# A spectral transformer block of eight batches: the second batch's attention begins beside the first batch's spectral part

## The chip, the cores and the metric

The kernel runs on one core of a Trainium2 chip. The metric is the device time of one execution in microseconds; of the kernel before the median of three runs is given. The engines are TensorE (PE, with its weight loads as PEld), VectorE (DVE), ScalarE (ACT), GpSimd (POOL) and SyncE (SP), whose queue issues the transfers. Each works off its own queue in order.

## The reference

```python
def _attn_ref(q, k, v, g_q, g_k):          # 8 batches, 12 heads, 448 positions, 64 per head
    q_n, k_n = rmsnorm(q, g_q), rmsnorm(k, g_k)
    scores = q_n @ k_n.transpose(0, 1, 3, 2) / sqrt(64)
    attn = exp(scores - max); attn = attn / (sum + 1e-9)
    return attn @ v

def _moe_ref(x, w_ch1, w_ch2):             # x: the heads side by side, 8 x 448 x 768
    mixed = real(fft(fft(x, axis=1), axis=2))
    u = x + mixed
    un = (u - mean(u)) / sqrt(var(u) + 1e-6)
    return u + relu(un @ w_ch1) @ w_ch2    # 768 x 3072 and 3072 x 768; both arrive as 64-bit floats
```

## The kernel before

A batch goes through four parts. **Attention** takes the heads in six pairs: normalise q and k (`norm_pair`), transpose them (`transpose_pair`, products `qk`), then four rows of scores of 112 positions each (`softmax_pair`: products `S`, minimum `mn`, exponential into `P`, sum, scaling), then transposes of `P` (`pt`, copied to SBUF as `T`) and products with the values (`av`) into `xT` (`value_pair`). **Spectral**: `fold` adds and subtracts halves and thirds of `xT` on VectorE (`eo`, `sd`, `tot`), `spectral` does the two transforms as products with the tables `D1` (products `y`, split into `Y`) and `D2` (products `ab`), adds transposes of `xT` (`x`) into `u` and normalises to `un`. **Input**: `ffn_input` transposes `un` into `unT`. **Feed-forward**: 24 `up` steps (products `h`, 18 each) and 36 `down` steps (products `o`, 12 each), 864 products a batch, in the order up 0, then six times four ups and six downs.

Most operands are split into a high and a low part, `A.copy` for the high and a subtraction for the low, so that three fast products stand for one exact one. In the first six pairs (batch 0) attention runs in plain 32-bit instead, without that split (`PLAIN_PAIRS`); the copies `T` of `pt` alternate there between VectorE and ScalarE.

The weights arrive in 64 bits. `convert` turns a tile into two 32-bit parts: a load into a raw slot (tile `dblw...`, slots `X`), two ScalarE steps (L653 into `magw...`, slot `M`; L654), three VectorE steps (L655, L659, L663), GpSimd's addition (L667), ScalarE's copy into the high part (L668), GpSimd's subtraction into the low part (L669). `Stream.converted` does a tile in two halves; there are two `M` slots of a whole tile each and four raw slots of half a tile. 60 tiles (24 for `up`, of 768 columns; 36 for `down`, of 512) are converted once and kept in DRAM: 14 during the first batch's attention and spectral part (`convert_some`, names with an `e`), the rest when `W1.load` or `W2.load` comes to them in the first feed-forward. Each stream has three buffers.

The program first issues all of batch 0's attention and spectral part. Then, for each batch, `merge` walks the feed-forward and, beside it, attention and spectral part of the next batch (`aux`): each `yield` carries a cost in ns, and the side advances until its costs reach a ratio of the main's. A scheduler with a time model of its own then moves instructions within each queue. `order` binds an instruction behind another: `pace` keeps the feed-forward's products in order, and `follow` puts batch 1's score products behind the last feed-forward product issued before them.

PSUM has eight banks: two for `ffn`, two for `S`, two for `PT`, one each for `av` and `q`; in batch 0 `y` uses `S` and `PT`, and `ab` uses `S`.

## Time and profile before

| | |
|---|---|
| median of 3 runs | 2242.81 us (2241.82 to 2243.02) |
| profiled execution, its own time | 2246.45 us |
| its span | 2244.7 us |
| TensorE busy | 2107.8 us (94%) |
| VectorE busy | 1630.5 us (73%) |
| ScalarE busy | 1074.2 us (48%) |
| GpSimd busy | 576.2 us (26%) |
| mean granted TensorE clock | 0.96 |

The profile is of one execution. Busy shares are means over parts with different limits: up to 197 us there is no feed-forward, from 197 to 546 us there is the first one with the conversion of the weights, and from there on seven feed-forwards with kept weights. A number after an instruction is its source line; operations called through a recording helper all have line 111 there, so they are told apart by the names of their tiles.

### The profile page before, as it was taken

The numbers are of one execution on the slowest core, as the hardware profiler recorded it, in microseconds if no ns is written. First come the engines' busy times: TensorE is split into PE (matmuls) and PEld (weight loads), VectorE is DVE, ScalarE is ACT, GpSimd is POOL, SyncE is SP. The second block draws the span as 40 slices with busy tenths as digits, with TensorE's granted clock in tenths as the row PEclk, the third lists the DMA queues.
The fourth block names the chain that finished last, engine by engine and source line by source line (L and its number), as shares of the span: only waits on it lengthen the run. The fifth ranks groups of instructions, "written<-read, shape, count | busy, mean of one in ns | idle before, by whom it ended". The sixth has DMA issues, their size and how long they took to land.

```text
span 2244.7 us, 32045 instructions
## 1 busy us (share of the span) xinstructions
PE 2107.8 (94%) x11164; PEld 1854.6 (83%) x11164; DVE 1630.5 (73%) x3281; ACT 1074.2 (48%) x2452; POOL 576.2 (26%) x442
## 2 busy tenths in 40 slices
PE   6887987769999999999999999999999999998997
PEld 3346866668999999999999999999999999998996
DVE  6896999888888577866788587867787588752122
ACT  5766776656554255524554355524554355421100
POOL 5883666854122021211121021101221022000000
PEclk7987988889999999999999999999999999999998
DMA  4556565557655575557655675558556674549664
GB/s 127 174 158 234 174 200 190 200 193 261 201 177 177 185 230 166 179 174 224 189 173 180 200 216 164 177 175 240 179 163 183 206 213 157 177 145 263 211 209 136
DMA packets 299188, 425.38 MB, mean 190 GB/s; under 512 B 187489, under 2 KB 225362, under 8 KB 299026
## 3 DMA queue, kind: packets, MB, share of 16 engines
q1 hardware_dynamic: 299026, 423.32, 61.0%
q8 instruction: 89, 1.46, 0.3%
q14 instruction: 73, 0.60, 0.1%
HBM read 363.47 MB, written 65.27 MB: 191 GB/s over the span
## 4 chain that ended last, share of the span: by engine, by line
PE 79%; DVE 9%; DMA 3%; ACT 2%; issue 2%; POOL 2%; SPq 0%; DVEq 0%; POOLq 0%; ACTq 0%
PE h L853 29%; PE o L874 28%; PE S L350 6%; PE av L439 4%; PE pt L427 4%; PE qk L313 1%; DMA w<-w 1%; PE y L530 1%; DVE mn L111 1%; DVE magw L663 1%; DMA dblw<-w 1%; PE oT L819 1%; DVE T L111 1%; DVE magw L655 1%; PE un L765 1%
## 5 line engine op out<-in xcount | busy, mean ns | idle before, releaser
L874 PE MATMUL o<-hs,w 128*128 128x448 f32 x3456 | 801.7, 374 | 24.5 <-DVE magw L655 6.8
L853 PE MATMUL h<-unT,w 128*128 128x448 f32 x3456 | 782.7, 371 | 6.0 <-POOL w L669 5.4
L874 PEld LDWEIGHTS o<-hs,w 128*128 128x128 f32 x3456 | 646.1, 191 | 84.0 <-ACT w L668 10.2
L853 PEld LDWEIGHTS h<-unT,w 128*128 128x128 f32 x3456 | 639.8, 189 | 59.7 <-POOL w L669 6.1
L111 ACT ACTIVATE P<-S,mn 112x448 f32<-112x448 f32 x384 | 243.1, 634 | 214.4 <-DVE mn L111 200.8
L111 POOL TENSOR_TENSOR qkn<-raw 112x1024 f32<-112x1024 f32 x47 | 89.8, 1912 | 731.1 <-PE qk L313 558.4
L111 DVE TENSOR_REDUCE mn<-S 112x1 f32<-112x448 f32 x384 | 233.3, 617 | 49.4 <-PE S L350 46.3
L111 ACT ACTIVATE hs<-h 128x448 fp32r<-128x448 f32 x192 | 104.4, 544 | 291.3 <-PE h L853 290.4
L111 DVE TENSOR_TENSOR acc<-o,acc 128x448 f32<-128x448 f32 x240 | 148.9, 621 | 109.5 <-PE o L874 107.8
L111 DVE SCALAR_TENSOR_TENSOR hs<-h,hs 128x448 fp32r<-128x448 f32 x192 | 119.3, 622 | 128.7 <-ACT hs L111 126.8
L439 PE MATMUL av<-T,vhl 128*128 128x448 f32 x504 | 179.9, 391 | 21.1 <-DVE T L111 11.6
L111 ACT CAST T<-pt 128x448 fp32r<-128x448 f32 x252 | 132.9, 533 | 135.3 <-PE pt L427 133.2
L111 POOL TENSOR_TENSOR ss<-ss,nhalf 112x16 f32<-112x16 f32 x48 | 150.0, 3125 | 112.9 <-DVE ss L111 109.6
L111 DVE TENSOR_TENSOR T<-pt,T 128x448 fp32r<-128x448 f32 x252 | 154.7, 617 | 27.8 <-ACT T L111 26.4
L111 DVE TENSOR_SCALAR P<-P,sm 112x448 f32<-112x448 f32 x336 | 158.0, 504 | 4.4
L427 PE MATMUL pt<-ident,P 112*128 112x112 f32 x1008 | 146.8, 262 | 1.5 <-DVE acc L111 1.5
L111 POOL TENSOR_TENSOR rstd<-st,nhalf 112x1 f32<-112x1 f32 (+2 forms) x32 | 18.5, 577 | 489.3 <-DVE st L111 489.3
L427 PEld LDWEIGHTS pt<-ident,P 112*128 112x128 f32 x1008 | 122.9, 143 | 23.0 <-DVE acc L111 2.1
L350 PE MATMUL S<-KD,QT 128*112 128x448 f32 x352 | 137.8, 393 | 2.0 <-ACT KD L111 1.6
L350 PE MATMUL S<-KL,QT 128*112 128x448 f32 x352 | 131.5, 376 | 2.6 <-DVE KL L111 2.5
L439 PEld LDWEIGHTS av<-T,vhl 128*128 128x128 f32 x504 | 95.7, 192 | 32.8 <-DVE T L111 14.9
L667 POOL TENSOR_TENSOR magw<-magw,dblw 128x256 uint32<-128x256 uint32 (+1 forms) x92 | 87.2, 956 | 73.6 <-DVE magw L663 50.4
(121 smaller groups left out, 2689.2 us busy)
## 6 DMA issues: line engine op xcount, KB each, us to landing
w<-w SPq DMA_DIRECT2D x288, 512.0 KB, 4.1
w<-w SPq DMA_DIRECT2D x192, 768.0 KB, 4.4
dblw<-w SPq DMA_DIRECT2D x60, 256.0 KB, 2.9
dblw<-w SPq DMA_DIRECT2D x32, 384.0 KB, 3.9
raw<-q SPq DMA_DIRECT2D x96, 112.0 KB, 4.3
raw<-k SPq DMA_DIRECT2D x96, 112.0 KB, 3.9
v<-v SPq DMA_DIRECT2D x96, 96.0 KB, 3.5
u_dram<-u SPq DMA_DIRECT2D x24, 336.0 KB, 3.5
```

The costliest lines, as they stand in the source:

```text
L111: ins = emit(*args, **kwargs)
L313: nc.tensor.transpose(pt[:, c * C : (c + 1) * C], qk[:, i, c].rearrange("t h d -> t (h d)"), ident[:C, :C],)
L350: ins = nc.tensor.matmul(s_, QT[:, h, cs], K[:, h], start=step == 0, stop=step == 1)
L427: nc.tensor.transpose(pt[:, c * C : (c + 1) * C], Pc[c][:, 512 * h + j * 128 : 512 * h + (j + 1) * 128], ident[:C, :C],)
L439: nc.tensor.matmul(av[:, :S], lv, T[:, i], start=(j == 0 and i == 0), stop=False)
L530: nc.tensor.matmul(o, src[:, par, t0 : t0 + n], D1[:, ri, par, cols], start=i != 1, stop=i != 0,)
L655: behind(nc.vector.tensor_scalar(out=value, in0=value, scalar1=MIN_HIGH, scalar2=MAX_HIGH, op0=ALU.max, op1=ALU.min,))
L663: behind(nc.vector.scalar_tensor_tensor(out=bits, in0=high, scalar=0xC0000000, in1=bits, op0=ALU.bitwise_and, op1=ALU.bitwise_or,))
L667: behind(nc.gpsimd.tensor_tensor(out=bits, in0=bits, in1=low, op=ALU.add))
L765: nc.tensor.transpose(pt[:, OFFS[i] : OFFS[i] + LENS[i]], uns[i][:, p * 128 : (p + 1) * 128], ident[: LENS[i], : LENS[i]],)
L853: pace(nc.tensor.matmul(o, w[:, a, c], unT[c][:, z], start=n == 0, stop=n == 17))
L874: pace(nc.tensor.matmul(o, w[:, a, f], hs[4 * g + f][:, z], start=n == 0, stop=n == 11))
```

## The change

Five things are edited. (1) The side work of batch 1 starts early: while batch 0 is in its spectral part, each of its steps is followed by two steps of batch 1, up to 14 (`AHEAD`). These 14 steps hold the four rows of scores of batch 1's first pair, and the transposes of q of its second. (2) `follow` now applies to all of batch 1's side products but the transposes of attention, and two `yield`s of 7000 and 1500 ns are added in its spectral part. (3) The transform's tables are loaded at step 40 of batch 0 instead of after its first step, the second one in two transfers; the gains' loads are issued in front of the first pair's. (4) In the plain pairs all copies `T` go to ScalarE. (5) A weight tile is converted whole: raw slots are twice as wide and two instead of four. `KL` and `D2` share one tile, and `xT` is allocated later.

```diff
+DFT_STEP = 40
+AHEAD = 14
...
-    def follow(ins):
-        order(
-            ins, paced[-1], mybir.DependencyClass.NoSync, mybir.DependencyReason.DATA
-        )
+    def follow(b, ins):
+        if b == 1 and paced:
+            order(
+                ins, paced[-1], mybir.DependencyClass.NoSync,
+                mybir.DependencyReason.DATA,
+            )
...
-    SLOTS = {"P": 8, "PT": 6, "X": 4, "M": 2, "unT": 6, "h": 6}
+    SLOTS = {"P": 8, "PT": 6, "M": 2, "unT": 6, "h": 6}
+    def wide(name, dtype=F32):
+        return sb.tile([128, 1800], dtype, tag="X", name=name, bufs=2)
...
         st = slot("PT", "d2s")[:N1, : 4 * N1].rearrange("s (n t) -> s n t", n=4)
-        nc.sync.dma_start(st, d2.rearrange("s (n t) -> s n t", n=4))
+        for r in rows_of(N1):
+            nc.sync.dma_start(st[r], d2[r].rearrange("s (n t) -> s n t", n=4))
...
-                    if (h * 3 + j) % 2 == 0:
-                        V.tensor_copy(T, pt[:, :S])
-                    else:
-                        A.copy(T, pt[:, :S])
+                    A.copy(T, pt[:, :S])
...
+                if b == 1:
+                    yield 400
                 for i in range(2):
-                    nc.tensor.matmul(
+                    follow(b, nc.tensor.matmul(
                         av[:, :S], lv, T[:, i], start=(j == 0 and i == 0), stop=False
-                    )
-                yield 800
+                    ))
+                yield 400 if b == 1 else 800
...
         a_, b_, c_ = EO
+        if b == 1:
+            yield 7000
...
             yield 980
+            if b == 1:
+                yield 1500
             for mirror in range(2):
...
-        raw = slot("X", f"dbl{name}", U32)[:, : c * f].rearrange(
+        raw = wide(f"dbl{name}", U32)[:, : c * f].rearrange(
...
-            for c in (slice(0, self.n // 2), slice(self.n // 2, self.n)):
-                convert(
-                    src[:, c], bits[:, c], [hl[:, k, c] for k in range(2)],
-                    f"{self.tag}{name}_{c.start}",
-                )
+            convert(src, bits, [hl[:, k] for k in range(2)], f"{self.tag}{name}")
...
+    load_gains()
     load_pair(0, 0)
-    load_gains()
     warm()
-    side = aux(0)
-    next(side)
-    load_dft()
-    for _ in side:
-        convert_some(CONVERT_EARLY)
+    second = aux(1)
+    ahead = iter(range(AHEAD if nb > 1 else 0))
+    for n, _ in enumerate(aux(0)):
+        if n == DFT_STEP:
+            load_dft()
+        if mixing:
+            for _ in range(2):
+                if next(ahead, None) is not None:
+                    next(second)
+        if n:
+            convert_some(CONVERT_EARLY)
...
-            aux(b + 1) if b + 1 < nb else iter(()),
+            second if b == 0 else aux(b + 1) if b + 1 < nb else iter(()),
```

`mixing` gets an entry when `aux` of a batch passes from attention to the spectral part. The products `y`, `x` and `ab` are wrapped in `follow` like `av`.

How the built queues move, at three places. The head of VectorE's queue; `0_0` is batch 0, pair 0. Before:

```order
L111 TENSOR_REDUCE ss0_0_139<-qkn0_0_137 112x16
L111 TENSOR_TENSOR raw0_0_110<-raw0_0_110,gneg_75 112x512
L111 TENSOR_SCALAR ss0_0_139<-ss0_0_139 112x16
L111 TENSOR_TENSOR D2_78<-d2s_159,D2_78 113x4x113
L111 TENSOR_TENSOR qkn0_0_137<-raw0_0_110,ss0_0_139 112x2x4x64 x2
L111 TENSOR_TENSOR QT0_0_163<-qk0_0_0_165,QT0_0_163 64x448 x2
```

and in the changed kernel:

```order
L113 TENSOR_REDUCE ss0_0_137<-qkn0_0_135 112x16
L113 TENSOR_TENSOR raw0_0_112<-raw0_0_112,gneg_75 112x512
L113 TENSOR_SCALAR ss0_0_137<-ss0_0_137 112x16
L113 TENSOR_TENSOR qkn0_0_135<-raw0_0_112,ss0_0_137 112x2x4x64 x2
L113 TENSOR_TENSOR QT0_0_156<-qk0_0_0_158,QT0_0_156 64x448 x2
```

The subtraction that makes the low part of `D2` no longer stands between the mean squares `ss` and the scaling `qkn`.

ScalarE's queue where the first batch's `Y` are copied (first two digits of `Y`: batch, real or imaginary; of `P`, `mn`, `S`: batch, pair, row). Before:

```order
L668 CAST w1e5_1379<-magw1e5_1380 128x384 x2
L668 CAST w1e6_1468<-magw1e6_1469 128x384 x2
L111 CAST Y0_0_0_1498<-y0_0_0_1491 113x390
L654 ACTIVATE dblw2_6_0_2185<-dblw2_6_0_2185 128x256
L111 CAST Y0_0_1_1508<-y0_0_1_1501 112x390
L654 ACTIVATE dblw2_6_2_2195<-dblw2_6_2_2195 128x256
L111 CAST Y0_1_0_1518<-y0_1_0_1511 113x390
L111 CAST Y0_1_1_1528<-y0_1_1_1521 112x390
L111 COPY bs0_0_1539<-ab0_0_1_1535 113x390
```

and in the changed kernel:

```order
L694 CAST w1e5_1269<-magw1e5_1270 128x768
L113 ACTIVATE P1_0_0_1371,sm1_0_0_1373<-S1_0_0_0_1374,mn1_0_0_1372 112x448
L113 CAST Y0_0_0_1368<-y0_0_0_1361 113x390
L113 CAST Y0_0_1_1395<-y0_0_1_1388 112x390
L694 CAST w1e6_1348<-magw1e6_1349 128x768
L113 ACTIVATE P1_0_0_1371,sm1_0_0_1373<-S1_0_0_1_1375,mn1_0_0_1372 112x448
L113 ACTIVATE P1_0_1_1398,sm1_0_1_1400<-S1_0_1_0_1401,mn1_0_1_1399 112x448
L680 ACTIVATE dblw2_6_2107<-dblw2_6_2107 128x512
L113 ACTIVATE P1_0_0_1371<-P1_0_0_1371,sm1_0_0_1373 112x448
L113 ACTIVATE P1_0_1_1398,sm1_0_1_1400<-S1_0_1_1_1402,mn1_0_1_1399 112x448
L113 CAST Y0_1_0_1422<-y0_1_0_1415 113x390
L113 CAST Y0_1_1_1432<-y0_1_1_1425 112x390
```

Exponentials and scalings of batch 1's first rows stand among the `Y` casts, and the step on the raw tile `dblw2_6` has moved from behind the first cast to behind the second.

VectorE's queue around one weight tile of the first feed-forward, `w1_10`. Before:

```order
L111 RECIPROCAL sm1_2_0_2317<-sm1_2_0_2317 112x2
L655 TENSOR_SCALAR magw1_10_2503<-magw1_10_2503 128x384 x2
L111 TENSOR_SCALAR P1_2_0_2315<-P1_2_0_2315,sm1_2_0_2317 112x448
L659 TENSOR_SCALAR magw1_10_2503<-magw1_10_2503 128x384 x2
L111 TENSOR_TENSOR xT1_1752<-av1_0_1_2114,xT1_1752 64x448
L663 SCALAR_TENSOR_TENSOR magw1_10_2503<-dblw1_10_0_2504,magw1_10_2503 128x384
L111 TENSOR_TENSOR R1_1_2382<-rem1_1_2377,R1_1_2382 64x448
L663 SCALAR_TENSOR_TENSOR magw1_10_2503<-dblw1_10_3_2514,magw1_10_2503 128x384
L111 TENSOR_TENSOR T1_1_0_0_2393<-pt1_1_0_0_2388,T1_1_0_0_2393 128x448
```

and in the changed kernel:

```order
L113 TENSOR_TENSOR T1_1_1_0_2379<-pt1_1_1_0_2374,T1_1_1_0_2379 128x448
L681 TENSOR_SCALAR magw1_10_2405<-magw1_10_2405 128x768
L685 TENSOR_SCALAR magw1_10_2405<-magw1_10_2405 128x768
L113 TENSOR_SCALAR sm1_2_3_2307<-sm1_2_3_2307 112x2
L689 SCALAR_TENSOR_TENSOR magw1_10_2405<-dblw1_10_2406,magw1_10_2405 128x768
L113 RECIPROCAL sm1_2_3_2307<-sm1_2_3_2307 112x2
```

Six instructions with three others among them have become three with one.

## Rows read from the trace of the kernel before

**Rows 1.** Stretches: us, busy us of each engine (instructions), PEclk, DMA share, GB/s.

```profile
20.00:154.00 134.00, 114.38 (x416) 49.69 (x416) 121.60 (x254) 106.09 (x264) 103.95 (x76) 0.84 0.53 158
154.00:197.00 43.00, 22.61 (x101) 19.22 (x102) 31.20 (x62) 16.86 (x36) 24.32 (x20) 0.58 0.56 183
197.00:237.00 40.00, 40.00 (x214) 36.25 (x214) 28.34 (x60) 30.33 (x71) 14.90 (x13) 0.98 0.66 215
237.00:500.00 263.00, 200.29 (x946) 171.54 (x945) 241.76 (x468) 177.50 (x423) 180.30 (x167) 0.86 0.59 192
500.00:546.00 46.00, 42.24 (x228) 37.18 (x227) 39.67 (x96) 30.35 (x76) 25.04 (x34) 1.00 0.80 283
546.00:795.00 249.00, 249.00 (x1392) 227.98 (x1391) 188.48 (x382) 116.74 (x263) 39.14 (x22) 1.00 0.62 189
```

The engines stand in the order PE, PEld, DVE, ACT, POOL.

**Rows 2.** Timeline, 5 to 21 us: start, us, engine, line, operation [idle before, releaser].

```profile
5.84 0.39 SPq L191 DMA_DIRECT2D d2s<-d  x1
...
10.82 2.93 POOL L111 TENSOR_TENSOR ss<-ss,nhalf 112x16 f32<-112x16 f32 x1 [8.72 <-DVE ss L111]
18.63 0.57 ACT L111 CAST D<-d2s 113x452 fp32r<-113x452 f32 x1 [16.61 <-DMA d2s<-d]
...
19.78 1.29 DVE L111 TENSOR_TENSOR qkn<-raw,ss 112x512 f32<-112x512 f32 x2
```

**Rows 3.** Groups, 20 to 154 us: count, busy us, mean ns of one, idle before.

```profile
L111 ACT ACTIVATE P<-S,mn 112x448 f32<-112x448 f32 x48 | 30.2, 631 | 10.4 <-DVE mn L111 10.3
L111 DVE TENSOR_REDUCE mn<-S 112x1 f32<-112x448 f32 x48 | 28.5, 614 | 1.5 <-PE S L347 1.4
...
L111 DVE COPY T<-pt 128x448 f32<-128x448 f32 x18 | 11.1, 616 | 6.2 <-PE pt L396 6.2
...
L111 ACT COPY T<-pt 128x448 f32<-128x448 f32 x18 | 9.5, 527 | 1.4 <-PE pt L396 1.3
```

**Rows 4.** Timeline of VectorE, 369 to 397 us: single instructions and pairs.

```profile
370.04 0.49 DVE L659 TENSOR_SCALAR magw<-magw 128x256 uint32<-128x256 uint32 x2
...
390.31 0.35 DVE L655 TENSOR_SCALAR magw<-magw 128x384 f32<-128x384 f32 x1
...
396.18 0.61 DVE L655 TENSOR_SCALAR magw<-magw 128x384 f32<-128x384 f32 x2
```

**Rows 5.** Timeline of ScalarE in the spectral part of batch 0.

```profile
173.62 0.43 ACT L654 ACTIVATE dblw<-dblw 128x256 uint32<-128x256 uint32 x1 [2.81 <-DMA dblw<-w]
...
174.91 0.85 ACT L111 CAST Y<-y 113x390 fp32r<-113x390 f32 x2
```

**Rows 6.** From the chain of waits: one run of feed-forward products.

```profile
542.98 2.45 PE o L874 x12
```

**Rows 7.** Groups, 237 to 500 us: GpSimd's addition and ScalarE's step on the raw tile.

```profile
L667 POOL TENSOR_TENSOR magw<-magw,dblw 128x256 uint32<-128x256 uint32 x42 | 37.5, 902 | 28.5 <-DVE magw L663 19.1 <-DMA raw<-k 4.4 <-DVE sm L111 2.6
...
L667 POOL TENSOR_TENSOR magw<-magw,dblw 128x384 uint32<-128x384 uint32 x32 | 36.1, 1133 | 31.1 <-DVE magw L663 25.6 <-ACT w L668 2.3 <-ACT dblw L654 1.5
...
L654 ACT ACTIVATE dblw<-dblw 128x256 uint32<-128x256 uint32 x41 | 17.8, 437 | 14.0 <-DMA dblw<-w 12.3 <-DVE qkn L111 0.9 <-DVE eo L111 0.6
```

**Rows 8.** Timelines of ScalarE and GpSimd: tile w1_10 from first to last, and a wait.

```profile
259.46 0.98 ACT L653 ACTIVATE magw<-dblw 128x384 f32<-128x384 f32 x2
...
270.12 2.10 POOL L669 TENSOR_TENSOR w<-magw,w 128x384 fp32r<-128x384 f32 x2
...
489.12 0.44 ACT L653 ACTIVATE magw<-dblw 128x256 f32<-128x256 f32 x1 [1.23 <-POOL w L669]
```

**Rows 9.** The page's transfers: count, KB each, median us to landing.

```profile
dblw<-w SPq DMA_DIRECT2D x60, 256.0 KB, 2.9
dblw<-w SPq DMA_DIRECT2D x32, 384.0 KB, 3.9
```

**Rows 10.** Waits of TensorE, 237 to 500 us: total, times, longest.

```profile
PE y L530 <- DVE eo L111: 14.7, 1, 14.7
```

More of the change, by code (lines that the diff above doesn't have):

```diff
@@ L165, in rows_of @@
         return [slice(a, z) for a, z in ((0, n - n % 16), (n - n % 16, n)) if a < z]
-    KL = cpool.tile([128, 2, S], F32R, name="KL")
+    rounded = cpool.tile([128, 2 * S + 8 * N1], F32R, name="rounded")
+    KL = rounded[:, : 2 * S].rearrange("r (h t) -> r h t", h=2)
     G.memset(KL.bitcast(F32), 0.0)
@@ L199, in spectral_block @@
     X_BANKS = (("either", "either"), ("either", "either"))
-    FOLD_SLOTS = (("unT", "unT"), ("PT", "P"), ("M", "X"))
+    FOLD_SLOTS = (("unT", "unT"), ("PT", "P"), ("M", None))
     loaded = {}
@@ L352, in softmax_pair @@
                     )
-                    if b == 1 and step == 0 and paced:
-                        follow(ins)
+                    if step == 0:
+                        follow(b, ins)
             for h, s_ in enumerate(banks):
@@ L448, in value_pair, with attention @@
         A.copy(xT[:, p, S : S + 1], xT[:, p, 0:1])
-    def attention(b, xT, EO):
+    xTs = {}
+    def attention(b, EO):
         yield from transpose_pair(b, 0)
@@ L468, in attention @@
             if p > 3 and b != 1:
-                fold(b, p - 4, xT, EO)
+                fold(b, p - 4, xTs[b], EO)
                 yield 0
-            values = value_pair(b, p, Pc, xT)
+            if p == 0:
+                xTs[b] = sb.tile([128, NR, S + 2], F32, tag="xT", name=f"xT{b}", bufs=1)
+            values = value_pair(b, p, Pc, xTs[b])
             for x in ahead:
@@ L475, in attention @@
         for p in range(0 if b == 1 else 2, 3):
-            fold(b, p, xT, EO)
+            fold(b, p, xTs[b], EO)
             yield 0
     rstds = {}
+    halves = {}
     def fold(b, p, xT, EO):
@@ L487, in fold @@
         once = slot(short, f"sd{b}_{p}").rearrange("r (i e t) -> r i e t", i=2, e=2)
-        eo = slot(kept, f"eo{b}_{p}").rearrange("r (i t) -> r i t", i=2)
+        if kept is not None:
+            eo = slot(kept, f"eo{b}_{p}")
+        else:
+            if p % 2 == 0:
+                halves[b] = wide(f"eo{b}_{p}")
+            eo = halves[b][:, p % 2 * 900 : p % 2 * 900 + 900]
+        eo = eo.rearrange("r (i t) -> r i t", i=2)
         add(eo[:, 0, :449], xT[:, p, :449], xT[:, p + 3, :449])
@@ L561, in token_tile @@
                 for i in range(3):
-                    nc.tensor.transpose(
+                    follow(b, nc.tensor.transpose(
                         xp[:n, i * 128 : (i + 1) * 128], src[:, 3 * half + i], ident
-                    )
+                    ))
                 V.scalar_tensor_tensor(
@@ L602, in spectral @@
                 for x_, (a, z) in enumerate(((0, 0), (0, 1), (1, 0))):
-                    nc.tensor.matmul(
+                    follow(b, nc.tensor.matmul(
                         o, D2[:kk, i, t, a, :n], Y[i, c][:, z], start=x_ == 0, stop=x_ == 2
-                    )
+                    ))
                 ab.append(o)
@@ L626, in spectral_block @@
     uns = {}
+    mixing = []
     def aux(b):
-        xT = sb.tile([128, NR, S + 2], F32, tag="xT", name=f"xT{b}", bufs=1)
         EO, uns[b] = [], {}
-        yield from attention(b, xT, EO)
-        yield from spectral(b, xT, EO, uns[b])
+        yield from attention(b, EO)
+        mixing.append(b)
+        yield from spectral(b, xTs[b], EO, uns[b])
     NF = DFF // 128
```

6 lines of the change are left out of this document (3 added, 3 removed).

## The prediction

> **What bounds the kernel now.** I read the view by stretches first [rows 1]. From 546 us on the TensorE row is full: 249.00 of 249.00 us busy at a granted clock of 1.00, and the next batch reads the same. The change leaves them alone: the built order on TensorE is that of before from product 1,122 of the feed-forwards' 6,912 on, and from 546 us up to that one only the sequence of the same products differs. So the end moves by what happens in the first 546 us, microsecond for microsecond. A feed-forward with the next batch's work beside it takes 249 us there; the first one takes 349 (197 to 546). That 100 us, and what can be had from the 197 before it, is all there is.
>
> Inside those stretches [rows 1] shows who is busy. From 20 to 154 us (attention of the first batch) VectorE has 121.60 of 134 us, ScalarE 106.09, GpSimd 103.95. From 237 to 500 us VectorE has 241.76 of 263 and TensorE 200.29, at a granted clock of 0.86: between its two levels of 1.2 and 2.4 GHz, lower after idle times. Busy shares do not say who sets the pace of 237 to 500, so I looked at the conversion of the weights, whose tiles TensorE needs in order. The groups of this stretch hold 42 and 32 half tiles on GpSimd [rows 7], 37 tiles in 263 us, 7.1 us each. There are two `mag` slots, so a slot turns in 14.2 us. [rows 8] shows one turn: the first instruction at 259.46, the last ends at 272.22, 12.8 us later; and at 489.12 ScalarE stood idle with the next tile until GpSimd's last instruction on an older one. **The two `mag` slots set the pace of that stretch**, and a turn is mostly waiting in queues: for a tile of 384 columns its own path is about 6 us (0.98 for the pair on ScalarE, 2.10 for GpSimd's last pair [rows 8], one each of the five steps between at 0.35 to 1.13 [rows 4, 7]), by the same count 4.5 for 256 columns, 5.1 on average; 9.1 us is waiting.
>
> **The change part by part.**
>
> *The DFT table.* VectorE's queue holds the subtraction on `D2` ahead of the first `qkn`. The table was issued at 5.84 and landed at 18.63, and `qkn` began at 19.78 though GpSimd's `ss` had ended at 13.75 [rows 2]. In the new order the subtraction is gone from there. `qkn` can start at 13.8: **-6 us**, all on the path, since everything later hangs on it. At its new place two loads (112 rows and one) stand for one; the casts that use it come far behind, so I cost it at nothing. If the load were still 12.8 us long, ScalarE's next exponentials would wait, 6 us back.
>
> *Copies T to ScalarE, whole tiles for halves, first attention.* VectorE loses 18 copies, 11.1 us [rows 3]. Merging: a pair of 384 columns takes 0.61, a pair of 256 takes 0.49, one alone 0.35 [rows 4]; 128 columns are then 0.06 and the second instruction's 0.26 has 0.08 that is not columns. Three operations a tile, 12 tiles: 3 us. ScalarE gains 18 copies of 0.53 [rows 3], 9.5 us, less what merging saves there. So VectorE falls from 121.6 to about 108 and ScalarE rises from 106 to about 113 of 134. Ends: 0 (ScalarE takes over at once) and -14. VectorE is the fullest row, but only by 15 us: I take **-7**.
>
> *The second batch's first four rows of scores inside the first batch's spectral part.* They add eight reductions of 0.61 on VectorE and eight exponentials of 0.63 on ScalarE [rows 3], with their scaling some 9 us on each. Stretch 154 to 197 has 11.8 idle us on VectorE and 26.1 on ScalarE [rows 1], so the work fits; but it stands in the queues ahead of two of the four `Y` casts and shares the two S banks with `y` and `ab`. Against that, the load wait of 2.81 us that held the `Y` casts [rows 5] now stands behind two of them. Ends: 0 and +12 (four rows one after another at 3 us: product, reduction, exponential, scaling). I take **+4**, a third, for the idle time.
>
> *Start of the first feed-forward.* Until its product 138 (five `up`, four `down`) the weights are there and TensorE is full (197 to 237 us) [rows 1]; then tile w2_6 gets its buffer and the loop of conversions begins. The new order puts 29 more side products ahead of that point. At 0.204 us for a long one (12 in 2.45 [rows 6]) and half that for a transpose: **+4**; ends 0 and +6.
>
> *The loop of conversions, 237 to 500.* A merged tile has a longer path of its own: 6.3 us by the same steps at double width, 1.2 more. But fewer instructions stand between its own. I counted them in both built orders over 44 tiles: VectorE 3.6 before, 1.7 now; ScalarE 11.6 and 7.6; GpSimd 1.5 and 0.4; in all 58%. If the waiting falls with them, 9.1 becomes 5.3, a turn 11.6 instead of 14.2, and 18.5 turns give -48. The other end is the raw slots. Four halves become two whole ones, and a slot is reloaded only when GpSimd has read the whole tile. A load takes 2.9 us for 256 KB and 3.9 for 384 [rows 9]; by that slope a whole tile takes 4.9 or 6.9, 5.8 on average. Raw turn: 0.4 issue, 5.8 load, 4.1 own work up to GpSimd's read, 3.5 of the reduced waiting: 13.8, or -7. Until now loads came early: ScalarE waited for them 12.3 us in all in its largest group [rows 7]. I take the middle, **-28**.
>
> The Trainium skill, "Perfetto Trace Analysis", section "Optimizing Scalar/DVE Operations", says that where ScalarE or VectorE are not saturated but cause bubbles elsewhere, breaking instructions up may get work done sooner, and larger operations pay where the engine is saturated. It speaks against the merging if the loop is latency-bound. By it the loop term would be positive; the third rival below is that case in this kernel's rows.
>
> *The wait of `y` for the folds.* TensorE stood 14.7 us behind `y` [rows 10]. In the new order 12 more products precede it, 2.4 us. But the tile that the product behind `y` needs ended only near 500, so this wait lies on top of the loop's and I count nothing for it.
>
> *The end of the first feed-forward.* Its last `x` transposes now come after all 864 products; they came 48 earlier. Then two `u`, one `un`, the transposes and the first `unT` must run: 3 us of bubble at most, against 6 us of products that moved ahead of the feed-forward. From 500 on TensorE has 42.24 of 46 busy. Net **0**, ends -4 and +4.
>
> Sum: -6 - 7 + 4 + 4 - 28 = **-33 us**. The profiled execution took 2246.45 us (span 2244.7), so 2213 for one like it; it stands 3.6 above the median of 2242.81, from which the same sum gives **2210**.
>
> **The rivals.**
>
> *One, loop unchanged.* The load term and the waiting cancel; the other terms leave -5: 2238. For it: the raw turn of 13.8 is close to 14.2. Against: the VectorE queue is shorter for every step.
>
> *Two, the whole of it.* Waiting falls with the queue rows and the attention gains 12: -6 - 12 + 2 + 4 - 45 = -57, or 2186. For it: VectorE at 92% in the loop, where a little less work takes away much waiting. Against: loads.
>
> *Three, slower: the two wide raw slots become the bound.* If waiting up to GpSimd's read stays as it is (two thirds of 9.1, 6.0), a raw turn is 0.4 + 5.8 + 4.1 + 6.0 = 16.3, 2.1 more than now; 18.5 turns give +39, in all 2277 at worst. It decides as soon as a raw turn exceeds 14.5. For it: the load begins later and is longer. Against: [rows 7], loads hardly waited for.
>
> That the change does not do what it says is mostly excluded: the moved rows are in the built order. Only the part on ordering does little, 12 products at `y`.
>
> **How the numbers follow.** Forecast 0.52 (2196 to 2228 for it alone), rival one 0.17, two 0.24, three 0.07. A measurement can tell about 0.2%, 4.5 us. Rival one lies at that edge: of its 0.17 I give 0.10 to faster, 0.06 to no change and 0.01 to slower. Faster 0.86, within 0.2% 0.06, slower 0.08. The range of 8 in 10 leaves out three and the far ends of one and two: 2184 to 2237.
>
> **What would show it.** Right: the first `qk` near 14.5 us instead of 20.5; the first product of the feed-forward near 188 instead of 197; a turn of the `mag` slots near 12.7 us in the loop; the second feed-forward's first product near 513 instead of 546; TensorE full behind it. Wrong: ScalarE waiting for loads in most turns (rival three, or one); the spectral part longer by 10 us; a bubble of over 5 us before the second feed-forward; any difference after that point.

## The result and the profile after

The forecast was 2210 us, 2184 to 2237. Measured: **2254.2 us** median of four runs (2252.05 to 2255.32) against 2242.7 of the kernel before in the same session (2241.82 to 2243.02), a ratio of 1.0050 with a 95% interval of 1.0035 to 1.0065. The change costs 11.5 us. The profiled execution took 2254.03 us, its span is 2252.3.

The stretches of the kernel after, with the columns of [rows 1]:

```profile
20.00:154.00 134.00, 110.68 (x409) 47.67 (x408) 115.26 (x199) 106.91 (x241) 93.85 (x52) 0.84 0.53 159
154.00:197.00 43.00, 21.36 (x110) 18.29 (x110) 35.63 (x66) 22.86 (x45) 17.89 (x12) 0.70 0.41 132
197.00:237.00 40.00, 37.26 (x195) 33.01 (x194) 26.16 (x54) 26.81 (x59) 14.04 (x11) 0.93 0.70 232
237.00:500.00 263.00, 191.67 (x898) 167.45 (x896) 233.24 (x338) 158.34 (x299) 158.12 (x91) 0.86 0.58 193
500.00:546.00 46.00, 44.40 (x235) 40.34 (x236) 30.45 (x55) 21.63 (x40) 24.62 (x19) 0.93 0.74 257
546.00:795.00 249.00, 244.53 (x1361) 222.72 (x1360) 189.04 (x385) 117.16 (x262) 39.19 (x22) 0.99 0.61 184
```

Beside [rows 1]: every side engine has less to do from 237 to 500 us (VectorE 233.24 for 241.76, GpSimd 158.12 for 180.30), and TensorE got less done too (191.67 for 200.29). From 546 to 795 us TensorE is no longer full: 244.53 of 249.00. That is the bubble, which the prediction had put at 3 us at most, and at nothing in the sum.

Where the time went is seen best from the feed-forward products, which keep their order; product n is the start of the n-th one in the timeline of TensorE.

| | before, us | after, us | change | forecast |
|---|---|---|---|---|
| start to the first `x` of batch 0 (end of attention) | 154.7 | 151.8 | -2.9 | -13 |
| to product 1 (spectral part) | 42.0 | 46.4 | +4.4 | +4 |
| product 1 to 139 | 38.0 | 45.9 | +7.9 | +4 |
| 139 to 703 (loop of conversions) | 263.2 | 255.9 | -7.3 | -28 |
| 703 to 1100 (end of the first feed-forward, start of the second) | 118.8 | 130.2 | +11.4 | 0 |
| start to product 1100 | 616.7 | 630.2 | +13.5 | -33 |

Behind that point the difference stays at 11.6 to 13.2 us up to product 6,001; in the last feed-forward it falls to 8.5, where TensorE waited 6.0 us for weight loads before and 4.0 after. The spans differ by 7.6: the execution profiled before stands 3.6 above its median.

The head came out as forecast. Timeline of the kernel after, to set against [rows 2]:

```profile
10.68 2.93 POOL L113 TENSOR_TENSOR ss<-ss,nhalf 112x16 f32<-112x16 f32 x1 [8.58 <-DVE ss L113]
13.64 1.29 DVE L113 TENSOR_TENSOR qkn<-raw,ss 112x512 f32<-112x512 f32 x2 [3.12 <-POOL ss L113]
14.39 1.61 PE L323 MATMUL qk<-ident,qkn 112*128 112x112 f32 x8 [2.17 <-DVE qkn L113]
```

`qkn` starts when `ss` ends, and the first `qk` at 14.39.

The attention then loses three of these six microseconds. Its groups in the kernel after, for [rows 3]:

```profile
L113 ACT ACTIVATE P<-S,mn 112x448 f32<-112x448 f32 x48 | 30.3, 635 | 9.7 <-DVE mn L113 9.2
L113 DVE TENSOR_REDUCE mn<-S 112x1 f32<-112x448 f32 x47 | 28.1, 615 | 6.3 <-PE S L357 6.1
L113 ACT COPY T<-pt 128x448 f32<-128x448 f32 x36 | 19.1, 533 | 1.2 <-PE pt L406 1.0
```

VectorE now waits 6.3 us for scores, 1.5 before [rows 3], and TensorE's waits for `T` are all on ScalarE. TensorE's waits in 20 to 154 us (total, times, longest), of the kernel after:

```profile
PE av L413 <- ACT T L113: 9.5, 11, 2.5
```

and of the kernel before:

```profile
PE av L406 <- DVE T L111: 5.0, 3, 2.3
PE av L406 <- ACT T L111: 2.4, 2, 1.8
```

With two engines copying in turn TensorE waited 7.4 us for `T`; with one, 9.5. And VectorE's busy time fell by 6.3 us (121.60 to 115.26), not by the 14 of its missing work. VectorE and then GpSimd, 69 to 76 us in the kernel after:

```profile
69.59 1.77 DVE L113 TENSOR_SCALAR sm<-sm 112x2 f32<-112x2 f32 x1
...
71.59 1.78 DVE L113 TENSOR_SCALAR P<-P,sm 112x448 f32<-112x448 f32 x1
73.29 1.85 DVE L113 TENSOR_SCALAR sm<-sm 112x2 f32<-112x2 f32 x1
...
75.38 0.45 DVE L113 TENSOR_SCALAR P<-P,sm 112x448 f32<-112x448 f32 x1
...
68.19 3.14 POOL L695 TENSOR_TENSOR w1e<-magw1e,w1e 128x768 fp32r<-128x768 f32 x1 [2.18 <-ACT w1e L694]
71.29 1.82 POOL L693 TENSOR_TENSOR magw1e<-magw1e,dblw1e 128x768 uint32<-128x768 uint32 x1
73.08 2.04 POOL L113 TENSOR_TENSOR qkn<-raw 112x1024 f32<-112x1024 f32 x1
```

Two numbers per row (`sm`, 112x2) took 1.77 and 1.85 us, where the shortest of these 24 took 0.15, and a `P` 1.78 where the next takes 0.45. The kernel before has such stalls too, the longest `sm` at 1.98 us. The two `sm` end within 0.03 us of the end of the GpSimd instruction beside them (71.33 and 75.12); the `P` ends 0.26 behind one (73.11). A GpSimd step on 768 columns lasts about 2 us, on 384 about 1.1 [rows 7], so a stall behind a merged one is longer. An estimate of the whole, from the traces: over 25 to 148 us, what each VectorE instruction took above the fast quarter of its own kind adds up to about 25 us before, 24 to 27 in the kernels with halves below, 29 to 32 in those with whole tiles, and 26 to 28 in e5, whole tiles with the copies on both engines. The Trainium skill, "SBUF — State Buffer", section "Terms", says that VectorE and GpSimd arbitrate for a shared port pair, which one of them holds for its whole instruction while the other is blocked; the two `sm` above, which end when GpSimd's instruction ends, agree.

In the loop ScalarE waits for loads. Its two first steps on a tile, 237 to 500 us, in the kernel after:

```profile
L679 ACT ACTIVATE magw<-dblw 128x768 f32<-128x768 f32 x16 | 14.5, 906 | 21.3 <-DMA dblw<-w 21.1 <-POOL w L695 0.2
L679 ACT ACTIVATE magw<-dblw 128x512 f32<-128x512 f32 x21 | 13.9, 667 | 11.2 <-DMA dblw<-w 7.0 <-POOL w L695 4.2
L680 ACT ACTIVATE dblw<-dblw 128x768 uint32<-128x768 uint32 x15 | 13.6, 908 | 1.7 <-DMA dblw<-w 1.6
L680 ACT ACTIVATE dblw<-dblw 128x512 uint32<-128x512 uint32 x20 | 13.4, 671 | 12.2 <-DMA dblw<-w 12.1
```

and in the kernel before, beside the row of 128x256 in [rows 7]:

```profile
L653 ACT ACTIVATE magw<-dblw 128x256 f32<-128x256 f32 x42 | 16.9, 430 | 5.2 <-POOL w L669 4.2 <-DMA dblw<-w 0.9
L654 ACT ACTIVATE dblw<-dblw 128x384 uint32<-128x384 uint32 x30 | 16.8, 558 | 1.7 <-DMA dblw<-w 1.5
```

Waits for `dblw<-w`: 21.1 + 7.0 + 1.6 + 12.1 = 41.8 us for 12.3 + 0.9 + 1.5 = 14.7. The loads are not the slow part. The page after:

```profile
dblw<-w SPq DMA_DIRECT2D x30, 512.0 KB, 3.7
dblw<-w SPq DMA_DIRECT2D x16, 768.0 KB, 4.8
```

They are shorter than the 4.9 and 6.9 that the prediction worked out from [rows 9]; they begin late, when GpSimd has read the whole tile. What the transfers' queue waited for in 237 to 500 us (total, times, longest), in the kernel after:

```profile
SPq L676 <- POOL magw L693: 72.2, 29, 7.1
```

and in the kernel before:

```profile
SPq L650 <- POOL magw L667: 105.8, 64, 7.0
```

In both, half of the loads in this stretch were issued 0.03 us behind the end of the addition that freed their slot. So raw slots held the loads back before the change too; with whole tiles ScalarE feels it. The `mag` slots, tile by tile, show the same: a slot is held 14.15 us by a `w1` tile and 9.88 by a `w2` tile (13.97 and 11.86 before), but stays empty 2.0 us between two tiles instead of 1.36.

The -7.3 of the table is not less waiting either. From product 139 to 703 TensorE has 382 side products (all that are not feed-forward) in the kernel before, 40 of the 48 `y` among them, and 294 in the one after, where all `y` come behind 703. Product 139 to 793, columns as in [rows 1], before and after:

```profile
234.70:522.70 288.00, 224.06 (x1073) 192.77 (x1071) 263.94 (x515) 193.34 (x465) 197.16 (x189) 0.87 0.60 197
```

```profile
244.10:528.10 284.00, 212.20 (x1005) 186.38 (x1004) 247.01 (x356) 165.41 (x313) 171.02 (x102) 0.86 0.59 200
```

TensorE is busy 11.9 us less, and it stands idle for 71.8 us instead of 63.9: the waiting that the prediction saw shrink has grown.

Last, the bubble. The chain of waits at the end of the first feed-forward in the kernel after (start, us, what):

```profile
545.09 0.48 DVE acc L113
...
546.68 0.96 DVE u L113 x4
547.64 0.02 issue
547.66 3.63 DMA u_dram<-u
...
551.37 0.94 ACT u L113 x2
552.31 0.83 ACT un L113
553.14 0.04 issue
553.19 0.60 PE un L787 x4
```

and ScalarE over the same microseconds:

```profile
547.92 0.94 ACT L113 ACTIVATE un<-u,st 112x768 f32<-112x768 f32 x1 [3.02 <-DVE st L113]
551.37 0.84 ACT L113 ACTIVATE u<-un 112x768 f32<-112x768 f32 x1 [2.52 <-DMA u_dram<-u]
...
552.22 0.92 ACT L113 ACTIVATE un<-u,st 112x768 f32<-112x768 f32 x1
```

The last two tiles of batch 1's spectral part come when no product of the first feed-forward is left. In before's chain that stretch is TensorE alone.

### The profile page after: what moved, and what is told of

Its sections match the earlier page's. It is cut to its first block, busy times and chain, and to the rows that moved or that the text cites. A ratio compares the mean times of both kernels' runs of the same rounds, so it can differ in the third digit from the quotient of the medians.

```text
span 2252.3 us, 31387 instructions
## 1 busy us (share of the span) xinstructions
PE 2104.8 (93%) x11164; PEld 1855.5 (82%) x11164; DVE 1622.0 (72%) x3083; ACT 1059.6 (47%) x2290; POOL 540.3 (24%) x322
## 4 chain that ended last, share of the span: by engine, by line
PE 71%; DMA 2%; DVE 1%; ACT 0%; issue 0%; SPq 0%; DVEq 0%; ACTq 0%
PE o L896 26%; PE h L875 26%; PE S L360 5%; PE av L448 4%; PE pt L434 4%; PE y L553 1%; PE qk L323 1%; DMA u_dram<-u 1%; PE oT L841 1%; DMA w<-w 1%; PE av L453 1%; PE un L787 1%; PE rem L394 1%; PE x L585 1%; PE ab L626 1%; DVE u L113 0%
## 5 line engine op out<-in xcount | busy, mean ns | idle before, releaser
L448 PE MATMUL av<-T,vhl 128*128 128x448 f32 x504 | 174.0, 381 | 4.3 <-DVE T L113 2.8
L113 DVE TENSOR_SCALAR P<-P,sm 112x448 f32<-112x448 f32 x336 | 165.7, 528 | 4.6
L360 PE MATMUL S<-rounded,QT 128*112 128x448 f32 x352 | 132.2, 377 | 1.8 <-DVE rounded L113 1.7
L113 DVE TENSOR_SCALAR sm<-sm 112x2 f32<-112x2 f32 x192 | 55.5, 289 | 54.9 <-ACT P L113 52.4
```

Of the source, the lines that this page charges most:

```text
L113: ins = emit(*args, **kwargs)
L360: ins = nc.tensor.matmul(s_, QT[:, h, cs], K[:, h], start=step == 0, stop=step == 1)
L448: follow(b, nc.tensor.matmul(av[:, :S], lv, T[:, i], start=(j == 0 and i == 0), stop=False))
```

## The experiments

The table holds what the kernels are compared by; an interval is the ratio's to the kernel before in the same session. That kernel's median was between 2240.9 and 2243.9 us in the sessions, so totals of different sessions are compared by their ratios. In brackets stand the side products on TensorE in a stretch, as the trace has them: only stretches with like numbers can be compared directly.

| kernel | median, us | ratio (95%) | product 1 | 139 to 703 | 139 to 793 | last `x` of batch 1 behind product | 793 to 1100 |
|---|---|---|---|---|---|---|---|
| before | 2242.7 | 1 | 196.7 | 263.2 (382) | 288.0 (415) | 816 | 94.0 |
| after | 2254.2 | 1.0050 (1.0035 to 1.0065) | 198.2 | 255.9 (294) | 284.0 (348) | 864 | 102.1 |
| e1 no yields | 2240.6 | 0.9983 (0.9966 to 0.9999) | 194.8 | 256.5 (348) | 281.7 (387) | 790 | 92.4 |
| e2 halves | 2244.3 | 1.0012 (1.0002 to 1.0021) | 200.4 | 247.2 (294) | 279.2 (348) | 864 | 102.7 |
| e3 no early start | 2251.2 | 1.0034 (1.0020 to 1.0048) | 193.1 | 254.4 (340) | 289.3 (388) | 864 | 105.6 |
| e4 only scores ordered | 2245.5 | 1.0010 (1.0000 to 1.0019) | 196.8 | 268.2 (381) | 290.6 (406) | 714 | 90.2 |
| e5 copies alternate | 2253.3 | 1.0051 (1.0036 to 1.0066) | 203.3 | 247.7 (294) | 276.5 (348) | 864 | 103.9 |
| e6 = e1 + e2 | 2232.3 | 0.9959 (0.9943 to 0.9975) | 199.3 | 249.2 (346) | 277.2 (384) | 792 | 90.8 |
| e7 = e1 + e3 | 2238.5 | 0.9986 (0.9972 to 1.0001) | 193.8 | 256.5 (340) | 289.8 (412) | 839 | 93.1 |
| e8 before, whole tiles | 2242.9 | 0.9996 (0.9981 to 1.0011) | 193.5 | 267.0 (376) | 292.2 (410) | 816 | 92.6 |
| e9 Square later | 2249.2 | 1.0032 (1.0017 to 1.0048) | 195.9 | 256.9 (294) | 284.5 (348) | 864 | 101.4 |
| e10 before, late table | 2250.3 | 1.0029 (1.0016 to 1.0043) | 192.1 | 268.7 (378) | 293.2 (408) | 864 | 104.5 |
| e11 before, copies | 2249.9 | 1.0023 (1.0011 to 1.0036) | 194.8 | 257.3 (336) | 290.6 (402) | 852 | 98.4 |
| e12 = e6, ratio 0.43 | 2235.8 | 0.9964 (0.9949 to 0.9979) | 199.8 | 249.3 (310) | 280.0 (368) | 816 | 91.3 |
| e13 = e6, ratio 0.46 | 2237.1 | 0.9962 (0.9949 to 0.9975) | 197.1 | 249.8 (349) | 283.9 (400) | 752 | 90.7 |
| e14 = e6, ratio 0.40 | 2243.1 | 0.9997 (0.9982 to 1.0012) | 197.0 | 244.2 (302) | 278.2 (356) | 864 | 101.1 |
| e15 = e2, three raw slots | 2258.3 | 1.0063 (1.0038 to 1.0087) | 205.9 | 250.4 (294) | 280.7 (348) | 864 | 105.6 |
| e16 before, 19 early tiles | 2247.5 | 1.0020 (1.0006 to 1.0033) | 215.3 | 240.9 (340) | 276.8 (414) | 816 | 94.4 |

A caution for single profiles: after, e1 and e9 have the same order on every engine up to product 676, yet reach product 139 at 244.1, 238.7 and 238.5 us. From 139 to 703 they agree within 1.0 us. So lengths of stretches carry the argument, and the medians.

**The two yields (e1).**

```diff
-        if b == 1:
-            yield 7000
...
-            if b == 1:
-                yield 1500
```

> The changed kernel without the two added yields of 7000 and 1500 ns in the second batch's spectral part; all else as changed. In its built order the last un transposes stand at product 840 of the first feed-forward instead of 868, so with 24 products of cover. Theory A (the spectral part of batch 1 was pushed to the very end, and its last tiles leave a bubble of some 9 us at the start of the second feed-forward): the time from product 841 to 881 falls from 20 us back to about 11, and the total to about 2245. Rival (the lost time is made in the conversion loop and before it, the bubble is only where it becomes visible): the products before 841 come later by what the bubble gives back, and the total stays at 2252 to 2256.

From product 841 to 881 it takes 12.6 us instead of 20.1, from 793 to 1100 92.4 instead of 102.1. The total falls by 0.67% of the time before, 15 us; 5.4 of them were there at product 139 already, in the same order, so about 10 are the edit's. The loop is as long (256.5), with 54 more side products in it. Theory A holds.

**Is it the place of the last `x`, or the yields themselves? (e14, e13, e12)** Three times the kernel of e6, with another `RATIO_FIRST`.

> The same kernel with RATIO_FIRST at 0.40, which puts the last x transposes at product 864 again and the last un at 868, as the two yields did. Theory: the bubble is back, 793 to 1100 takes 101 to 105 us against 90.8 in the sixth experiment, total 2239 to 2246. Rival (the yields themselves cost, not the place): 793 to 1100 below 95 us.

> The sixth experiment's kernel (no yields, halves) with RATIO_FIRST at 0.46: the last x transposes of batch 1 stand at product 752 of the first feed-forward, at 792 with 0.45. Theory (the bubble depends on their place behind product 864 and is gone by 840): product 865 to 883 stays at 4.3 to 5 us, 793 to 1100 at 90 to 91 us, total within 4 us of 2232. Rival (the earlier the side work ends, the better): 793 to 1100 below 88 us, total 2228 or less.

> The kernel without yields and with halves (the sixth experiment), with RATIO_FIRST at 0.43 instead of 0.45: batch 1's side work walks a little slower beside the first feed-forward. Theory (an early end of the side work is what saved the bubble; a slower side brings it back in part): 865 to 883 longer than 4.5 us, total 2232 to 2238. Rival (less side work in the conversion loop lets the conversions run faster): total 2229 or less.

e14 has no yields, and the bubble is back: 101.1 us. Windows of 5 us of e14, columns as in [rows 1]:

```profile
536.00:541.00 5.00, 1.87 (x13) 1.23 (x11) 1.02 (x6) 3.27 (x8) 0.54 (x1) 1.00 0.82 284
541.00:546.00 5.00, 4.52 (x20) 3.48 (x19) 4.97 (x13) 4.45 (x13) 0.54 (x1) 0.66 0.26 70
```

TensorE stands for 3.1 of the first five, and after the idle stretch its granted clock is 0.66 in the next, between its two levels of 1.2 and 2.4 GHz. e13 and e12 have `x` early and no bubble (90.7, 91.3). e12 keeps within its theory's numbers (865 to 883 takes 4.7 us) but brings no bubble back, as its last `x` still stand at 816. e13's total is 5 us above e6's, outside what the theory allowed, but in another session; their ratios are the same (0.9962 and 0.9959). Over all kernels the last column follows the one beside it: 90.2 to 94.4 us with the last `x` at 839 or before, 98.4 at 852, 101.1 to 105.6 at 864, with no exception in the table.

**The Square behind the next `un` (e9).**

```diff
-            A.activation(u, un, AF.Square, accum_out=st[:n, 3:4])
+            if late:
+                late.pop()(shifted)
+            if b == 1:
+                late.append(norm)
+            else:
+                norm()
```

`norm` holds the Square and what follows from it, and is ordered behind the `un` given to it.

> The changed kernel in which, for batch 1, each tile's Square is issued behind the next tile's un on ScalarE; the computation is the same, and TensorE's built order is that of the changed kernel. Theory (in the last spectral tiles each Square waits for the store of the tile that it overwrites, 2.7 and 3.6 us in the chain of waits, and holds up the next un behind it): product 865 to 883 takes 3 to 6 us less than the 8.0 of the changed kernel together with the products just before it, total 2248 to 2251. Rival (the bubble is the length of the last tiles' work alone): total within 1.5 us of the changed kernel's 2254.

The wait in the chain was real, and worth next to nothing. ScalarE in e9:

```profile
542.97 0.94 ACT L113 ACTIVATE un<-u,st 112x768 f32<-112x768 f32 x1 [3.82 <-DVE st L113]
...
545.70 0.93 ACT L113 ACTIVATE un<-u,st 112x768 f32<-112x768 f32 x1 [0.97 <-DVE st L113]
547.11 0.84 ACT L113 ACTIVATE u<-un 112x768 f32<-112x768 f32 x1 [0.48 <-DMA u_dram<-u]
```

The last `un` starts 2.73 us behind the one before, 4.30 in the kernel after; but 865 to 883 takes 8.5 us, where the theory wanted 2 to 5, and 793 to 1100 is 101.4. The total of 2249.2 lies in the theory's range for another reason: in the profiles the 5 us by which it is lower were there at product 139 already, in the same order, so they are not shown to be the edit's. The bubble is not this wait; that it is the length of the last tiles' own work, as the rival has it, fits, but rests on the chain above.

**Halves again (e2), whole tiles alone (e8), a raw slot less (e15).**

```diff
-            convert(src, bits, [hl[:, k] for k in range(2)], f"{self.tag}{name}")
+            for c in (slice(0, self.n // 2), slice(self.n // 2, self.n)):
+                convert(
+                    src[:, c], bits[:, c], [hl[:, k, c] for k in range(2)],
+                    f"{self.tag}{name}_{c.start}",
+                )
```

with four raw slots of half a tile; e15 is e2 with three; e8 is the opposite edit in the kernel before.

> The changed kernel with the weight tiles converted in halves again and four raw slots of half a tile; all else as changed. Theory A (whole tiles shorten the loop, by the 7 us that the loop gained between products 139 and 841): product 841 about 7 us later than in the changed kernel, total about 2261. Rival (two wide raw slots lengthen a turn, and only something else hides it): product 841 earlier by 5 us or more, total 2249 or less.

> The kernel before with the weight tiles converted whole and two wide raw slots, and nothing else changed. My forecast (less waiting in the queues, a turn of the mag slots shorter by 1.5 us): total about 2243 - 28 = 2215. Theory from the second experiment (a raw slot comes free later and its load is longer, so ScalarE gets the next tile later, 0.6 us a turn): the gap between a mag slot coming free and its next first instruction grows from 1.4 to about 2 us, the loop from product 139 to 793 is longer by 0 to 10 us, total 2243 to 2253.

> The second experiment's kernel (changed, tiles in halves) with three raw slots of half a tile instead of four; TensorE's order of the first two feed-forwards is unchanged. Theory (ScalarE gets the next raw tile late when raw slots come free late, which is what two wide slots cost): the gap between a mag slot coming free and its next first instruction grows from 1.2 us to 2 or more, a turn from 13.1 to 14 or more, product 793 at 530 or later, total 2252 or more. Rival (raw slots do not bind): within 3 us of 2244.

Halves shorten 139 to 703 by 8.7 us (255.9 to 247.2) with the same side products, and 139 to 793 by 4.8, as 3.9 are given back there; the total falls by 0.38%, 8.5 us. e6 against e1, the same edit with nearly the same side products, gains 4.5 up to 793. The empty time of a `mag` slot is 1.17 us in e2, a turn 13.1 (after: 2.0 and 13.75).

In the kernel before, whole tiles gain nothing (0.9996): the slot is held 1.5 us less by a `w2` tile, 1.0 more by a `w1` tile, and empty 0.6 to 0.8 longer; 139 to 703 is 3.8 us longer, 139 to 793 4.2.

e15 takes away one raw slot (the scheduler then orders the head a little otherwise too): empty time 1.8, a turn 13.55, 139 to 703 3.2 us longer than in e2 and 139 to 793 1.5. The direction is the theory's, its figures (2 us, 14 us, product 793 at 530; it came at 528.1) are not reached, and of the total's 0.51%, 11 us, most lies elsewhere: the attention ends 4.7 later (160.0 for 155.3).

So loads do wait for raw slots, and two whole ones cost 4 to 5 us up to product 793 in three pairs; that is less than the totals suggest. ScalarE's waits for loads in e6, 237 to 500 us:

```profile
L676 ACT ACTIVATE dblw<-dblw 128x256 uint32<-128x256 uint32 x42 | 17.8, 435 | 11.0 <-DMA dblw<-w 10.8 <-DVE magw L681 0.2
L675 ACT ACTIVATE magw<-dblw 128x384 f32<-128x384 f32 x32 | 17.1, 552 | 6.0 <-DMA dblw<-w 4.0 <-POOL w L691 1.8
L676 ACT ACTIVATE dblw<-dblw 128x384 uint32<-128x384 uint32 x30 | 16.6, 553 | 8.6 <-DMA dblw<-w 8.6
```

23.4 us in all, against 41.8.

**The early start and the ordering (e3, e7, e4).** e3 and e7: `AHEAD = 0`. e4: `follow` acts on the products `S` alone.

> The changed kernel with AHEAD = 0: batch 1's attention begins with the first feed-forward as before; all else as changed. Theory A (the four rows of scores and the side products that they pull forward cost 4 us in the spectral part and 8 us up to product 138): product 1 at about 194 us and product 138 at about 232, 12 us earlier than in the changed kernel; the side then has four rows more to do beside the loop, and its last un transposes stand at 868 as in the changed kernel, so some of it is given back: total 2244 to 2252. Rival (the early rows are free because they use idle time): product 138 moves by less than 3 us and the total is 2256 or more.

> The changed kernel without the two yields and with AHEAD = 0; tiles whole. The third experiment gave back 9 of its 12 us at product 138 up to the end. Theory (given back because its side work comes late into the last part of the first feed-forward, which the yields make worse): product 138 at about 232 us, the bubble at the second feed-forward 4 us or less, total about 2235. Rival (the early start of batch 1 is worth in the loop what it costs in front of it, with or without the yields): total within 3 us of the first experiment's 2240.6.

> The changed kernel with follow on the score products alone, as before the change; all else as changed. In its built order y stands at product 648 instead of 714 to 756 and the last un at 801 instead of 868. Theory A (the ordering of all side products is what pushes the spectral part to the end): the bubble at the second feed-forward goes, product 881 about 9 us earlier, total about 2245. Rival (products that are not ordered make TensorE wait for tiles that are late, y by 15 us or more): product 841 later by 5 us or more, total 2254 or more.

Without the early start product 139 comes at 232.2 and 233.0, 5 to 12 us earlier than in after, e1 and e9. But what was not done early is done late: 703 to 1100 takes 140.5 us in e3 (130.2 after) and 126.4 in e7 (117.6 in e1). e7's total, 0.9986, cannot be told from e1's 0.9983. e3 (1.0034) cannot be told from after (1.0050) either: as far as these pairs show, the early start only moves work. The ordering does more. Without it 87 side products come back into 139 to 703, which takes 12 us more (268.2), and 793 to 1100 takes 12 less (90.2); product 881 comes 2.6 us earlier and not 9, but the total is 0.40% lower, 9 us, which is theory A's 2245. With whole tiles and before's number of side products, e4's loop is 5 us longer than before's.

**The parts ahead of the feed-forward (e10, e11, e5).** e10 is the kernel before with `load_gains` in front, the table at step 44 in two transfers and `KL` and `D2` in one tile; e11 has all copies `T` on ScalarE; e5 is the changed kernel with the copies alternating.

> The kernel before with the first part of the change alone: gains in front of the first pair, the transform's tables loaded at step 44 of batch 0 and the second in two transfers (KL and D2 in one tile, xT allocated later). My forecast: 6 us gained at the first qk stay, first x of batch 0 near 149, first feed-forward product near 191, total 2237. Rival (attention loses them again on the way, as it did in the changed kernel): first qk near 14.5, first x within 2 us of 154.7, product 793 within 2 us of 522.7, total 2241 to 2245.

> The kernel before with the copies T of the plain pairs on ScalarE and nothing else changed. My forecast for these copies, with little from merging: the first x of batch 0 5 us earlier, near 150, and total about 2238. Rival (the first feed-forward ends when the last weight tile is converted and the last side work done, and what the attention gains is lost in the conversion loop): first x near 150, but product 793 within 3 us of 522.7 and total 2240 to 2246.

> The changed kernel with the copies T of the plain pairs alternating between VectorE and ScalarE again; all else as changed. The built order of TensorE is that of the changed kernel up to product 138. My forecast for this part (all copies on ScalarE shorten the first attention by 7 us): the first x transpose at about 159 us instead of 151.8, total about 2261. Rival (the moved copies load ScalarE, which then sets the pace, and cost what the merged conversion gained): the first x at 148 or earlier, total about 2249.

Each part alone makes the kernel before slower. e10 has 1.8 of its 6 us left at its first `x` (152.9) and 4.6 at product 1 (192.1), and loses 5.5 in the loop (268.7) and 10.5 at the end, where its last `x` fell to product 864. In e11 the attention ended at 157.3, later than the 154.7 of before, where forecast and rival both said 150, and `av` waited 12.0 us for `T`. Only beside the other edits are the copies a gain: in e5 the attention ends at 158.2, in after at 151.8, about what its expectation had from the forecast, though the total is no later (1.0051 for 1.0050). The 5 us that e5 thus reaches product 1 later are made up in the loop (247.7, with whole tiles).

**Five more tiles ahead of the loop (e16).** `CONVERT_EARLY = 0.16` in the kernel before.

> The kernel before with CONVERT_EARLY at 0.16: 19 weight tiles instead of 14 are converted beside the first batch's attention and spectral part, and five fewer in the first feed-forward. If the loop is bound by its own tiles at 7.1 us each, product 793 comes 35 us earlier less what five tiles cost in front of product 1 (between 0 and 35 us): total 2210 to 2243, with a loop from product 139 to 793 of 253 instead of 288 us. Rival (the first feed-forward is bound by something else, the side work's total): the loop stays above 275 us and the total is 2243 or more.

139 to 703 is shorter by 22.3 us, but the 40 `y` that stood in it have moved behind 703. Up to product 793 TensorE has the same work (414 side products for 415), and there five tiles fewer gain 11.2 us (276.8 for 288.0), 2.2 a tile and not 7.1; five more ahead of product 1 cost 18.6, 3.7 each. Both numbers of the rival hold, a loop above 275 us and a total above 2243. What else holds that stretch was not separated.

**Both faults undone (e6).**

> The changed kernel without the two yields and with the weight tiles in halves with four raw slots, the first two experiments together. If the two costs are apart (the bubble at the second feed-forward, and the raw slots in the loop), they add: 2254.2 - 13.6 - 9.9 = 2231, faster than both kernels. Rival (they are one cost seen twice, the end of the loop waits for the same tile): about 2241.

They add within the intervals: 0.9959 of the kernel before (0.9943 to 0.9975), 9 us faster, and 20 faster than the changed kernel; 0.9945 would be the exact sum. It beats both. Its stretches:

```profile
500.00:546.00 46.00, 44.32 (x242) 39.32 (x241) 42.11 (x104) 30.37 (x76) 22.85 (x32) 1.00 0.84 286
546.00:795.00 249.00, 248.50 (x1391) 227.93 (x1390) 187.78 (x378) 116.53 (x262) 39.34 (x22) 1.00 0.62 188
```

TensorE is nearly full across the seam.

## Why the prediction was wrong

At product 1100 forecast and profile lie 46.5 us apart: 20.7 of them in the loop, 11.4 at its end, 10.1 in the attention and 4.3 in the two stretches between.

- **The DFT table, -6.** Right where it was read: the first `qk` at 14.39. Wrong in "all on the path, since everything later hangs on it": in e10, which has this part alone, 1.8 of the 6 us are left at the end of the attention, and none at product 1100.
- **Copies and merging in the attention, -7.** The attention lost 3.2 us against the head. The step that failed is the reading of the fullest row: 15 us more busy than ScalarE did not make VectorE the bound, and with the copies alone (e11) the attention is 2.6 us longer. Nothing was counted for `av` waiting on one copying engine (12.0 us there for 7.4), nor for stalls behind longer GpSimd steps (about 25 to 30 us in sum). Beside the other edits the copies do gain 6.4 (e5), so these parts do not add, and how the loss divides among them stays open.
- **Scores in the spectral part, +4.** Right: +4.4 in the pair; without the early start (e3) the stretch takes 41.3 us, 5.1 less than after.
- **Start of the first feed-forward, +4.** +7.9 in the pair; 43.9 and 42.6 us in e1 and e9 make it +5 to +6. The mechanism was right (28 more side products, 29 were counted), the size somewhat low.
- **The loop, -28.** The largest miss, and the step that failed is "if the waiting falls with them": fewer instructions in the queues did not mean less waiting. TensorE's idle time from product 139 to 793 rose from 63.9 to 71.8 us, as ScalarE waited for loads that began late. The stretch's -7.3 equals the end of the range that the raw slots gave, but that is luck: the stretch holds 88 side products fewer. In no pair with like side products are whole tiles a gain: 139 to 703 is 3.8 us longer than before's in e8, and halves make the changed kernel's 8.7 shorter (e2), with 63.5 us of idle time up to 793. Nor had loads come early, as the prediction took from ScalarE's waits: in the kernel before, too, half of them were issued as soon as a slot came free. The prediction's two ends were two models, "waiting falls with the queue rows" and the raw turn; the second was worked out to be the longer turn and then averaged with the first. The third rival named the mechanism; its price was too high, as loads were shorter than estimated. The Trainium skill, "Perfetto Trace Analysis", section "Optimizing Scalar/DVE Operations", which the prediction cited against the merging (breaking work up may finish it sooner), describes what e2 did.
- **`y`, 0.** Right, and for the reason given. The 14.7 us of [rows 10] are gone, and TensorE waits for the tile instead. Of the kernel after:

```profile
474.04 1.11 PE L875 MATMUL h<-unT,w 128*128 128x448 f32 x2 [9.42 <-ACT w L694]
500.04 1.11 PE L896 MATMUL o<-hs,w 128*128 128x448 f32 x2 [11.82 <-ACT w L694]
```

- **The end of the first feed-forward, 0 (-4 to +4).** This step decided the sign: +11.4 from product 703 on, of which 8.1 behind 793, and without the yields (e1) the kernel is not slower than before (0.9983). The prediction had read the move of the last `x` from 816 to 864 correctly from the order, and priced it by one tile's path, "3 us of bubble at most". Its one long wait is indeed shorter (timeline of the kernel after):

```profile
553.19 0.60 PE L787 MATMUL un<-ident,un 112*128 112x112 f32 x4 [2.45 <-ACT un L113]
```

What it left out: two tiles in series, the side products still due (21 more than before from product 793 to 1100), and the granted clock after the idle time, 0.92 from 550 to 555 us and 0.74 from 555 to 560.

- **The claim on what bounds the kernel**, that two `mag` slots set the pace, is not borne out as a price. TensorE does wait for tiles to the end of the loop; but e16 shows that of the 7.1 us a tile only 2.2 leave with the tile up to product 793.

Not settled: why 139 to 703 is 5.5 us longer in e10, where the conversions are as before, and as short in e5, with whole tiles, as with halves (ScalarE waits 27.4 us for loads there, for 41.8). The built orders differ, and an order is worth some 5 to 8 us in this loop, as much as the price of whole tiles; that price rests on its sign in e2, e6 and e8 together, and e5 stands against it.

## What to carry to other kernels

When side work is moved in an order, first look at where its last instructions land against the next stage's first: 48 products of cover there were worth 8 to 11 us here, more than the changed kernel had gained in any stretch ahead of them. Before two lengths of a stretch are compared, count the work in it: here the shorter one held 88 products fewer and more idle time. A gain in front of a stage that shares its engines with the moved work is not a gain of the program until it is seen behind that stage. Before halves are merged, count the buffers they pass through: here fewer and larger slots of the same bytes made the next load wait for the whole tile.

## What the hardware showed unexpectedly

- The table's load of 113 rows was issued at 5.84 and its first reader ran at 18.63, after 16.61 us of idle time that the load ended [rows 2]. In two transfers, the 112 rows landed 3.8 us after issue in the kernel after, 3.5 in e9; for the single row the profile gives no landing. The place in the program changed too, so the split alone is not shown to be the cause.
- A VectorE instruction on two numbers a row, 0.15 us at its shortest, took 1.85 us beside GpSimd.
- The same order reached product 139 at 238.5 to 244.1 us in three executions: what the first 240 us give cannot be read from one profile to better than about 5 us.
